# Two more scheduling passes and 24 hand-given leads and delays in an attention and mixture kernel's order of issue

## The chip, the cores and the metric

The kernel runs on one core of a Trainium2 chip. A time is the device time of one execution in microseconds (us). The kernel before was run three times, and its median is what the changed kernel is held against.

## The reference

Inputs are q, k and v (8 batches, 8 heads, 576 positions, 64 channels) and four weight matrices. Two attentions are added, and the sum goes through a gated feed-forward layer:

```python
q_d = q.reshape(B, H, 144, 4, D).mean(axis=3)         # k_d, v_d alike
out_up = np.repeat(softmax(q_d @ k_d.T / 8) @ v_d, 4, axis=2)
mask = abs(pos[:, None] - pos[None, :]) < 4           # seven neighbours
out_local = softmax(where(mask, q @ k.T / 8, -1e9)) @ v
x = (out_up + out_local).transpose(0, 2, 1, 3).reshape(4608, 512)
y = ((x @ w1) * (x @ w2) @ w3) @ w_out                # 512 -> 1024 -> 1024 -> 512
```

## The kernel before, in words

**The work.** The two last weights are multiplied with each other once (`fold`): 16 blocks of w3 (`block m hf`) and 8 blocks of w_out (`out_weight j`) are loaded, turned into float32 in three steps by ScalarE and VectorE (`words`: lines 301, 309 or 313, and 316), and 64 products (`product m j`, line 351, two MATMUL records each) build the folded weight `wphl`; `part m hf` issues them and copies a finished eighth out (lines 371, 372). The w1 and w2 blocks are loaded the same way (`gate_weights`; tiles w1a, w2a, wo, wb) and kept as a high and a low part.

The attention of a batch has a pooled part (`pooled b`, with `quad b qd`: scores into s_ps at line 482, exponentials at line 496, scaling at line 508, transposes into t_ps at line 521; then values into o_ps at line 449) and a local part in three units for each batch. In batches 0 and 1 (`PB`) the local part runs on TensorE: `group_unit n` calls `group_scores b j qd` (se_ps, line 655), its inner `rest` makes the transposes te_ps (line 626) and calls `group_values n` (oe_ps, line 697). The pooled sums of these batches are made by `pooled_sums b`, which loads q in 4 and k in 8 transfers (lines 553, 582) and adds them on VectorE. In batches 2 to 7 the local part runs on VectorE, ScalarE and POOL (`unit n`, VectorE's 128x768 products at line 767).

Two units make a chunk of 384 tokens; `moe c` runs it: for each of 8 slices f of the hidden layer 24 matmuls of 128x384 into the two banks pab (three matmuls for one product, lines 269 to 271, in float32r), ScalarE's copy of the first bank (line 912), VectorE's product with the second (line 914), the split into gh and gl (lines 919, 921), and `down f`: nine matmuls of 128x512 into acc. The end of a chunk copies acc out and stores it (lines 929, 942). There are 12 chunks.

**The order.** Every step is a `Task` with an engine, an assumed cost, its inputs and the buffers that it takes (`Ring`). Nothing runs while the list is made. `Plan.run` is a list scheduler on this graph: each engine takes, of its tasks that can start within `slack` of the earliest one, the one with the smallest priority; forward from the start or backward from the end (`back=True`). `Plan.order` alternates backward and forward passes (the start times of the one, negated, are the priorities of the next), tries 192 forward schedules, replays each with random delays, and keeps the one with the best mean. The tasks are then issued in its order, and each engine executes its own instructions in that order and waits by semaphores:

```python
self.best = min(found, key=lambda f: f[:2])[2]
self.mean = min(found)[0]
return [self.tasks[i] for i in self.best[3]]
```

SyncE's queue (SP) issues all loads of weights and inputs in plan order; POOL issues the accumulating transfers. A weight load needs one of 4 raw buffers (`early_raw`), a pooled batch's k load one of 2 (`k4`). Engines run their queues independently of each other.

Of the kernel before, what the change touches and what calls it, by code (L numbers as in the profile page):

```python
# [9 lines left out]
F32 = mybir.dt.float32  # L10
# [50 lines left out]
SEEDS = 4  # L61
ROUNDS = 8
AHEAD = 4

LOWS = dict(early=('ACT', 'ACT', 'DVE'), late=('ACT', 'DVE'))


class Ring:

    def __init__(self, n):  # L70
        self.n, self.held = n, []
# [6 lines left out]


class Task:  # L80
    __slots__ = ("eng", "cost", "fn", "deps", "late", "rings", "after")

    def __init__(self, eng, cost, fn, deps, late, rings, after):
        self.eng, self.cost, self.fn, self.deps, self.late, self.rings, self.after = eng, cost, fn, deps, late, rings, after


class Plan:

    def __init__(self):
        self.tasks = []  # L90

    def add(self, eng, cost, fn, deps=(), take=(), uses=(), late=0.0):

        got, rings, after = [], [], []
        for r in take:
            held, old, last = r.take()
            got.append(held)
            rings.append(old)
            after += last[:1]
        t = Task(eng, cost, fn, [d for d in deps if d is not None], late, rings, after)  # L100
        for h in list(got) + list(uses):
            h.append(t)
        self.tasks.append(t)
        return (t, *got) if take else t
# [71 lines left out]
    def replay(self, order, seed):  # L176
# [13 lines left out]
            end[i] = x  # L190
        return max(end)

    def order(self):


        self.link()
        n = len(self.tasks)
        far = [0.0] * n
        for i in reversed(range(n)):
            far[i] = self.tasks[i].cost + self.tasks[i].late + max([far[j] for j in self.suc[i]], default=0.0)  # L200
        found = []
        self.log = []
        for slow, spare in SLOW:
            now = self.run([-x for x in far], 0.05, slow=slow, spare=spare)
            for _ in range(ROUNDS):
                back = self.run([-x for x in now[2]], 0.05, back=True, slow=slow, spare=spare)
                tried = [self.run([-x for x in back[2]], z, slow=slow, spare=spare) for z in SLACKS]
                now = min(tried, key=lambda r: r[0])
                self.log.append((slow, spare, round(now[0], 1), round(min(sum(self.replay(r[3], k) for k in range(SEEDS)) / SEEDS for r in tried), 1)))
                found += [(sum(self.replay(r[3], k) for k in range(SEEDS)) / SEEDS, len(found) + i, r) for i, r in enumerate(tried)]  # L210
        self.best = min(found, key=lambda f: f[:2])[2]
        self.mean = min(found)[0]
        return [self.tasks[i] for i in self.best[3]]


def dve_us(n, fast=False):
# [23 lines left out]
def tile_attention_moe(ctx: ExitStack, tc: tile.TileContext, q, kw, vw, qk4, v4, w1, w2, w3, wout, edge, out):  # L240
# [78 lines left out]
    wo, folded = [None], []  # L319
    wo_ready, wp_ready, g_ready = {}, {}, {}  # L320

    def out_weight(j):
        def place():
            if wo[0] is None:
                wo[0] = wpool.tile([128, NF, DM], F32R, name="wo").bitcast(F32)
            return wo[0][:, j]
        _, ld, wo_ready[j], _ = words(wout[j].unsqueeze(1), place, [], "early")
        early.append(wo_ready[j])

    def fold():  # L330

        accs, held, xs, last = {}, {}, {}, {}
        start = {}

        def block(m, hf):
            T, _, tx, h = words(w3[m, hf].unsqueeze(1), lambda: pools["early"].tile([128, 512], F32, name="w3", bufs=BUFS["w3"]), [R["w3"]], "early")
            xs[m, hf] = T, tx, h

        def product(m, j):
            T, tx, h = xs[m, j // 4]  # L340
            three_of = m // 5
            shared = m not in (3, 4)

            def prod():
                if j == 0:
                    if not shared:
                        accs[m] = ps.tile([128, DM], F32, tag="ab", name="accw", bufs=BUFS["ab"])
                    elif m % 5 == 0:
                        for i in range(3):
                            accs[m + i] = ps.tile([128, DM], F32, tag="acc", name=f"accw{i}")  # L350
                nc.tensor.matmul(accs[m], lhsT=T["x"][:, j % 4 * 128:j % 4 * 128 + 128], rhs=wo[0][:, j], start=j == 0, stop=j == NF - 1)  # L351
            deps = [tx, last.get(m), wo_ready[j], start.get(three_of) if shared else None]
            ring = R["acc" if shared else "ab"]
            if j == 0 and (not shared or m % 5 == 0):
                t, held[m] = add("PE", 4 * mm_us(DM), prod, deps, take=[ring], uses=[h])
                if shared:
                    start[three_of] = t
                    held[m + 1] = held[m + 2] = held[m]
            else:
                t = add("PE", 4 * mm_us(DM), prod, deps, uses=[h, held[m]])  # L360
            last[m] = t

        def part(m, hf):
# [24 lines left out]
    def gate_weights(g):  # L388

        pool, users = ("early", early) if g < 2 else ("late", late)  # L390
        before = [] if g < 2 else list(early)
        n = 512 if g == 0 else 256
        at = (g - 1) * n if g else 0
        parts = 512 // n
        for wi, wsrc in enumerate((w1, w2)):
            for k0 in range(0, KT, parts):
                src = wsrc[min(g, 1), k0:k0 + parts, :, at:at + n].rearrange("k p n -> p k n")
                T, ld, tx, wx = words(src, lambda: pools[pool].tile([128, nw], F32, name="wx", bufs=BUFS[pool + "_wx"]), [R[pool + "_wx"]], pool, parts)
                ld.deps += before

                def high(T=T, wi=wi, k0=k0):
                    if gates[wi][g] is None:
                        both = [wpool, pools.get("wlate")][g - 1].tile([128, 2, KT, 2, n], F32R, name=["wo", "wb"][g - 1])
                        for i in range(2):
                            gates[i][g] = both[:, i]
                    T["p"] = gates[wi][g][:, k0:k0 + parts]
                    nc.scalar.copy(out=T["p"][:, :, 0], in_=T["x"].rearrange("p (k n) -> p k n", k=parts))
                th = add("ACT", act_us(nw), high, [tx] + (folded if g == 1 else []), uses=[wx])
                tl = add("DVE", dve_us(nw), lambda T=T: nc.vector.tensor_tensor(out=T["p"][:, :, 1], in0=T["x"].rearrange("p (k n) -> p k n", k=parts), in1=T["p"][:, :, 0].bitcast(F32), op=ALU.subtract), [th], uses=[wx])
                users += [th, tl]  # L410
                g_ready.setdefault((wi, g), []).extend([th, tl])


    oups, oup_ready, oup_held, raws = {}, {}, {}, {}
    pep = []

    def pooled(b):
        P = {}
        if b in PB:
# [48 lines left out]

    def quad(b, qd, P, lq, hq, hpt):
        T = {}

# [64 lines left out]

    fours, four_ready = {}, {}

    def pooled_sums(b):

        fours[b], four_ready[b] = {}, []
# [49 lines left out]
        pep.extend(done)  # L593
        return add("Pool", 0.0, lambda: None, done), hq

    def group_unit(n):
        b, j = divmod(n, NJ)
        c, u = divmod(n, 2)
# [16 lines left out]
        pep.extend(lvs)  # L615
        quads = [group_scores(b, j, qd, starts) for qd in range(2)]

        def rest():
            hpt = None
            pts = []  # L620
            for qd, (U, hs, no) in enumerate(quads):
# [18 lines left out]
            group_values(n, T, pts, hpt, lvs, hvs)  # L640
        return rest

    def group_scores(b, j, qd, starts):

        U = {}
# [36 lines left out]
        no = [add("DVE", dve_us(n2), lambda: nc.vector.tensor_tensor(out=p3(), in0=p3(), in1=wide_(U["sm"]), op=ALU.mult), [t], uses=[hs])]  # L682
        return U, hs, no

    def group_values(n, T, pts, hpt, lvs, hvs):

        b, j = divmod(n, NJ)
# [47 lines left out]
    chunks, x_ready, x_held = {}, {}, {}  # L735
    nq, nk = UT * D, (UT + W - 1) * D

    def unit(n):
        b, j = divmod(n, NJ)
        c, u = divmod(n, 2)  # L740
# [125 lines left out]
    per = lambda f: 4 if f < 4 else 2  # L866
    out_v = out.rearrange("(b k t) m -> b t k m", k=NB, t=BT)

    def moe(c):
        T = {}  # L870
        gated = []
# [17 lines left out]
                    lastd = add("PE", 3 * mm_us(DM), mmul, d, uses=[hg, hacc])  # L889

        for f in range(NF):
            ends, banks = [], []
            for which in range(2):
                t = None
# [27 lines left out]
            lag.append((f, [th, tl], hg))  # L922

        for f, d, hg in lag:
            down(f, d, hg)
        for i in range(3):
            def store_h(i=i):
# [27 lines left out]
    for n in range(NU):  # L955
        scores(n + 1)
        if n in rests:
            rests[n]()
        else:
            if n % NJ == 0:  # L960
                pooled(n // NJ)
            unit(n)
# [114 lines left out]
```

## Time and profile before

| what | value |
|---|---|
| three runs | 782.77, 783.5, 785.19 us; median 783.5 us |
| profiled execution | 783.63 us, of which the span from first to last instruction is 781.9 us |
| TensorE matmul (PE) busy | 752.5 us, 96% of the span |
| TensorE weight load (PEld) busy | 654.8 us, 84% |
| VectorE (DVE), ScalarE (ACT), POOL busy | 613.0, 540.0, 115.8 us |
| TensorE's mean granted clock | 0.993 of full speed |

The 1.7 us between span and time lie around the instructions. Busy shares are means over stages that differ, so the wait that ends last in a stage counts there. The matmuls' ends are modelled: a matmul of 128x384 is shown as 0.34 us long while the next starts 0.17 to 0.18 us later, so idle time between matmuls appears slightly too small.

### The profile page before, as it was taken

The page shows a single profiled execution, that of the slowest core. Times are in us where ns is not written, and L with a number is a line of the kernel's source. Part 1 is how long each engine was busy: PE and PEld are TensorE (multiplying, and loading weights), DVE is VectorE, ACT ScalarE, POOL GpSimd, SP SyncE. Part 2 cuts the span into 40 slices and gives each one's busy share as a digit, 9 for nine tenths or more (in the row PEclk, how much of TensorE's full clock was granted, in tenths as well). Part 3 has the DMA queues.
Part 4 walks back from the last instruction along what each step waited for, and adds up shares of the span by engine and source line. Part 5 has one row for each costly group of instructions (what it writes and reads, how often), then busy time and mean ns, then how long its engine had stood idle before and what let it go on. Part 6 is the DMA issues. An engine that isn't in the chain of part 4 may idle for free.

```text
span 781.9 us, 15058 instructions
## 1 busy us (share of the span) xinstructions
PE 752.5 (96%) x5320; PEld 654.8 (84%) x5320; DVE 613.0 (78%) x1049; ACT 540.0 (69%) x2120; POOL 115.8 (15%) x139
## 2 busy tenths in 40 slices
PE   4889999999999999999999999999999999999995
PEld 1445588898999899999999999998999999999994
DVE  4457966749999999989999998998998998963110
ACT  5788898647978688666787686776785787841211
POOL 1000011000221122211121222110221220110000
PEclk9999999999999999999999999999999999999998
DMA  8995779433576727856549739854469544350101
GB/s 291 305 252 182 230 190 218 81 104 103 117 181 177 149 63 202 202 99 171 127 88 224 172 80 216 169 119 135 119 134 224 122 114 120 63 100 1 41 0 41
DMA packets 42548, 111.92 MB, mean 143 GB/s; under 512 B 5080, under 2 KB 11224, under 8 KB 42472
## 3 DMA queue, kind: packets, MB, share of 16 engines
q0 software_dynamic: 12672, 38.94, 28.9%
q1 hardware_dynamic: 29800, 72.01, 28.5%
q8 instruction: 42, 0.69, 0.4%
q14 instruction: 34, 0.28, 0.1%
HBM read 80.26 MB, written 9.44 MB: 115 GB/s over the span
## 4 chain that ended last, share of the span: by engine, by line
PE 73%; issue 7%; DMA 7%; DVE 6%; ACT 5%; POOL 1%; SPq 1%; POOLq 0%; ACTq 0%; DVEq 0%
PE pab L269 14%; PE pab L270 14%; PE pab L271 14%; PE acc L269 7%; PE acc L271 7%; PE acc L270 7%; PE accw L351 3%; DMA raw<-in_w_dram 3%; PE t_ps L521 2%; DMA raw<-in_wout_dram 2%; PE o_ps L449 2%; ACT pexp L496 1%; DVE pr L767 1%; DMA xl<-pv 1%; PE s_ps L482 1%
## 5 line engine op out<-in xcount | busy, mean ns | idle before, releaser
L777 ACT ACTIVATE junk<-pr 128x64 f32<-128x64 f32 x432 | 110.8, 257 | 19.0 <-DVE pr L767 8.4
L767 DVE TENSOR_TENSOR pr<-q_t,kv 128x768 f32<-128x768 f32 x126 | 119.8, 973 | 3.6 <-DMA kv<-in_kw_dram 3.5
L826 ACT ACTIVATE pv<-kv,s_t 128x64 f32<-128x64 f32 x432 | 114.5, 342 | 10.3 <-DVE s_t L803 5.9
L269 PE MATMUL acc<-wphl,gh 128*128 128x512 f32 x288 | 115.5, 401 | 0.0
L271 PE MATMUL acc<-wphl,gl 128*128 128x512 f32 x288 | 113.8, 395 | 0.0
L270 PE MATMUL acc<-wphl,gh 128*128 128x512 f32 x288 | 113.6, 394 | 0.0
L912 ACT COPY a<-pab 128x384 f32<-128x384 f32 x96 | 45.9, 478 | 79.9 <-PE pab L271 66.5
L914 DVE TENSOR_TENSOR a<-pab,a 128x384 f32<-128x384 f32 x96 | 53.2, 554 | 53.5 <-PE pab L271 48.8
L842 POOL DMA_DIRECT2D xl<-pv x54 | 47.2, 875 | 311.4 <-DVE xl L844 249.7
L919 ACT CAST gh<-a 128x384 fp32r<-128x384 f32 x96 | 49.2, 513 | 59.4 <-PE acc L270 52.1
L780 DVE TENSOR_REDUCE s_t<-pr 128x12 f32<-128x768 f32 x90 | 84.1, 944 | 0.1
L777 ACT ACTIVATION_READ_ACCUMULATOR junk<-pr 128x1 f32 x432 | 81.1, 188 | 0.0
L351 PE MATMUL accw<-wo,w 128*128 128x512 f32 x128 | 64.4, 638 | 15.5 <-DVE w L316 12.2
L921 DVE TENSOR_TENSOR gl<-a,gh 128x384 fp32r<-128x384 f32 x96 | 53.9, 562 | 27.9 <-ACT gh L919 27.5
L834 DVE TENSOR_TENSOR pv<-kv,s_t 128x768 f32<-128x768 f32 x72 | 69.8, 979 | 0.1
L269 PE MATMUL pab<-xh,wo 128*128 128x384 f32 x192 | 66.3, 346 | 0.5 <-ACT a L912 0.5
L269 PE MATMUL pab<-xh,w2a 128*128 128x384 f32 x192 | 66.1, 344 | 0.3 <-DVE a L914 0.2
L269 PE MATMUL pab<-xh,w1a 128*128 128x384 f32 x192 | 66.2, 345 | 0.0
L269 PE MATMUL pab<-xh,wb 128*128 128x384 f32 x192 | 65.8, 343 | 0.2
L270 PE MATMUL pab<-xl,w2a 128*128 128x384 f32 x192 | 65.7, 342 | 0.0
L271 PE MATMUL pab<-xh,w2a 128*128 128x384 f32 x192 | 65.5, 341 | 0.0
L271 PEld LDWEIGHTS acc<-wphl,gl 128*128 128x128 f32 x288 | 54.1, 188 | 13.2
(109 smaller groups left out, 1718.6 us busy)
## 6 DMA issues: line engine op xcount, KB each, us to landing
xl<-pv POOLq DMA_DIRECT2D x54, 384.0 KB, 4.3
raw<-in_w_dram SPq DMA_DIRECT2D x32, 512.0 KB
qks<-in_qk_dram POOLq DMA_DIRECT2D x18, 576.0 KB, 7.4
kv<-in_kw_dram SPq DMA_DIRECT2D x18, 576.0 KB
kv<-in_vw_dram SPq DMA_DIRECT2D x18, 576.0 KB
vs<-in_v_dram POOLq DMA_DIRECT2D x24, 288.0 KB, 6.5
q_t<-in_q_dram SPq DMA_DIRECT2D x18, 384.0 KB
out_dram<-o_sb SPq DMA_DIRECT2D x24, 256.0 KB
```

The lines of the kernel that those rows point to most:

```text
L269: nc.tensor.matmul(out_ps, lhsT=lh, rhs=rh, start=first, stop=False)
L270: nc.tensor.matmul(out_ps, lhsT=lh, rhs=rl, start=False, stop=False)
L271: nc.tensor.matmul(out_ps, lhsT=ll, rhs=rh, start=False, stop=last)
L351: nc.tensor.matmul(accs[m], lhsT=T["x"][:, j % 4 * 128:j % 4 * 128 + 128], rhs=wo[0][:, j], start=j == 0, stop=j == NF - 1)
L767: (nc.gpsimd if o in share["qk_pool"] else nc.vector).tensor_tensor(out=T[o], in0=T["q"], in1=T["k"][:, o * D:o * D + nq].rearrange("p (t ...
L777: nc.scalar.activation(out=junk, in_=T[o][:, t], func=AF.Copy, accum_out=T["s"][:, t, o:o + 1])
L780: reds.append(add("DVE", dve_us(nq), lambda o=o: nc.vector.tensor_reduce(out=T["s"][:, :, o], in_=T[o], op=ALU.add, axis=AX.X), [tp], uses ...
L826: nc.scalar.mul(out=T["pv", o][:, tt], in_=T["v"][:, (tt + o) * D:(tt + o + 1) * D], mul=T["s"][:, tt, o:o + 1])
L834: nc.vector.tensor_tensor(out=T["pv", o], in0=T["v"][:, o * D:o * D + nq].rearrange("p (t d) -> p t d", d=D), in1=T["s"][:, :, o].unsqueez ...
L914: tg = add("DVE", dve_us(CT), lambda f=f: nc.vector.tensor_tensor(out=T["a", f], in0=T["p", 1, f], in1=T["a", f], op=ALU.mult), [ta, ends[ ...
L919: nc.scalar.copy(out=T["gh", f], in_=T["a", f])
L921: tl = add("DVE", dve_us(CT), lambda f=f: nc.vector.tensor_tensor(out=T["gl", f], in0=T["a", f], in1=T["gh", f].bitcast(F32), op=ALU.subtr ...
```

## The change

Each planning function is wrapped (`@plan.named`), so that every task carries the name of its group: the function and its whole-number arguments, with " SP" added for tasks of the SP engine; in `moe` the group is set by hand to `gates c f` and `down c f`. The body of the loop in `gate_weights` becomes a function, `gate_block g wi k0`, with the same tasks. `rest` gets n as an argument for its name alone. After the best of the 192 schedules is chosen as before, its start times become priorities; twice a forward pass, a backward pass (with 10% more transfer time) and a set of shifts follow: a negative number gives a group's tasks a lead, a positive one a delay. A last forward pass makes the order that is issued. No task, cost, buffer or instruction is added, removed or altered.

```diff
+SHIFTS = [
+    "",
+    "gates_0_1:4.5",
+    "block_0_1:14.5 block_1_1:-1 down_0_1:-7 down_0_2:-2.5 gate_block_0_0_2:-2.5 gate_block_2_0_0:8 gates_0_3:-6"
+    " group_scores_0_2_1:-3 group_scores_1_0_0:-11 group_scores_1_1_0:-19 group_scores_1_2_1:-3 group_values_2:-26.5"
+    " out_weight_4:-3 part_4_1:-2 pooled_2:2 pooled_sums_1_SP:-14 product_5_0:-1.5 product_6_4:-6.5 product_7_4:29"
+    " quad_0_1:3.5 quad_1_0:-13.5 quad_1_1:-7 rest_4:0.5",
+]
...
+        self.group = group + " SP" if eng == "SP" else group
...
+    def named(self, fn):
+
+        def run(*a):
+            old, self.group = self.group, " ".join([fn.__name__] + [str(x) for x in a if isinstance(x, int)])
+            r = fn(*a)
+            self.group = old
+            return r
+        return run
...
+    def again(self, prio):
+        now = self.run(prio, 0.1)
+        back = self.run([-x for x in now[2]], 0.05, back=True, slow=1.1)
+        return [-x for x in back[2]]
+
...
         self.mean = min(found)[0]
-        return [self.tasks[i] for i in self.best[3]]
+
+        prio = list(self.best[1])
+        for k, line in enumerate(SHIFTS):
+            if k:
+                prio = self.again(prio)
+            shift = dict((g.replace("_", " "), float(x)) for g, x in (w.split(":") for w in line.split()))
+            prio = [p + shift.get(t.group, 0.0) for p, t in zip(prio, self.tasks)]
+        self.final = self.run(prio, 0.1, slow=1.1)
+        return [self.tasks[i] for i in self.final[3]]
...
+            plan.group = f"gates {c} {f}"
...
+            plan.group = f"down {c} {f}"
...
-            rests[n]()
+            rests[n](n)
```

## Rows read from the trace of the kernel before

**Rows 1.** The page: busy time of each engine, share of the span, instructions
```profile
PE 752.5 (96%) x5320; PEld 654.8 (84%) x5320; DVE 613.0 (78%) x1049; ACT 540.0 (69%) x2120; POOL 115.8 (15%) x139
```
**Rows 2.** Windows: stretch, its length, busy time by engine, granted clock, DMA share, GB/s
```profile
0.00:8.31 8.31, 0.00 (x0) 0.00 (x1) 1.50 (x3) 3.96 (x6) 3.67 (x19) 1.00 0.73 259
8.31:46.00 37.69, 30.80 (x112) 12.71 (x112) 22.20 (x60) 25.93 (x63) 1.82 (x2) 1.00 0.98 302
46.00:98.00 52.00, 50.41 (x545) 27.21 (x546) 39.56 (x96) 43.83 (x121) 0.83 (x1) 1.00 0.71 213
98.00:106.00 8.00, 6.24 (x38) 5.25 (x40) 4.15 (x10) 7.74 (x21) 0.83 (x1) 0.79 0.81 256
106.00:200.00 94.00, 92.94 (x1073) 83.29 (x1066) 67.25 (x149) 68.85 (x267) 9.40 (x10) 1.00 0.50 126
200.00:560.00 360.00, 359.52 (x2278) 330.68 (x2277) 334.66 (x513) 272.25 (x1195) 72.80 (x78) 1.00 0.65 148
560.00:760.00 200.00, 200.00 (x1227) 184.78 (x1226) 141.50 (x219) 113.74 (x448) 26.41 (x28) 1.00 0.42 97
740.00:760.00 20.00, 20.00 (x105) 18.52 (x104) 3.35 (x6) 2.98 (x6) 0.00 (x0) 1.00 0.00 0
760.00:781.90 21.90, 12.56 (x63) 10.85 (x61) 2.23 (x4) 3.75 (x7) 0.00 (x0) 0.83 0.14 37
```
**Rows 3.** Timeline of PE, 13 to 47 us: start, length, what, [idle before <-releaser]
```profile
13.31 3.74 PE L351 MATMUL accw<-wo,w 128*128 128x512 f32 x4 [1.22 <-DVE wo L316]
18.73 7.13 PE L351 MATMUL accw<-wo,w 128*128 128x512 f32 x16 [1.68 <-DVE w L316]
...
28.82 5.42 PE L351 MATMUL accw<-wo,w 128*128 128x512 f32 x12 [2.06 <-DVE wo L316]
...
41.02 3.98 PE L351 MATMUL accw<-wo,w 128*128 128x512 f32 x8 [0.92 <-DVE w L316]
46.26 1.13 PE L351 MATMUL accw<-wo,w 128*128 128x512 f32 x2 [1.25 <-DVE w L316]
```
**Rows 4.** Timeline of the DMA issues on SP, 4 to 13 us and 78 to 84 us
```profile
4.30 7.67 SPq L582 DMA_DIRECT2D k<-in_qk_dram  x8
12.13 0.33 SPq L294 DMA_DIRECT2D raw<-in_w_dram  x1
...
78.77 2.08 SPq L582 DMA_DIRECT2D k<-in_qk_dram  x4
...
82.42 1.77 SPq L582 DMA_DIRECT2D k<-in_qk_dram  x4
```
**Rows 5.** Timeline of PE, 98 to 102 us
```profile
99.99 0.39 PE L521 MATMUL t_ps<-ident,pexp 112*72 112x112 f32 x2 [1.23 <-ACT pexp L508]
100.91 1.21 PE L521 MATMUL t_ps<-ident,pexp 112*72 112x112 f32 x10 [0.53 <-ACT pexp L508]
```
**Rows 6.** Timeline of ACT, 98 to 102 us
```profile
98.99 0.64 ACT L407 CAST w2a<-wx 128x512 fp32r<-128x512 f32 x1
99.50 1.97 ACT L508 ACTIVATE pexp<-pexp,grs 128x144 f32<-128x144 f32 x6
101.34 0.63 ACT L407 CAST w2a<-wx 128x512 fp32r<-128x512 f32 x1
```
**Rows 7.** Windows of tile pab alone, columns PE, PEld, DVE, ACT, clock, DMA
```profile
101.90:105.70 3.80, 3.80 (x12) 3.37 (x12) 0.00 (x0) 0.50 (x1) 0.55 1.04 357
106.60:108.80 2.20, 2.20 (x12) 2.20 (x13) 0.00 (x0) 0.00 (x0) 1.00 0.76 180
```
**Rows 8.** Groups by line on DVE: busy us, mean ns, idle before, releasers
```profile
L767 DVE TENSOR_TENSOR pr<-q_t,kv 128x768 f32<-128x768 f32 x126 | 119.8, 973 | 3.6 <-DMA kv<-in_kw_dram 3.5
...
L914 DVE TENSOR_TENSOR a<-pab,a 128x384 f32<-128x384 f32 x96 | 53.2, 554 | 53.5 <-PE pab L271 48.8 <-ACT junk L777 3.1 <-ACT a L912 0.9
```
**Rows 9.** Timeline of ACT, 770 us to the end
```profile
771.20 1.28 ACT L929 COPY o_sb<-acc 128x512 f32<-128x512 f32 x2 [1.62 <-PE acc L271]
775.90 0.58 ACT L929 COPY o_sb<-acc 128x512 f32<-128x512 f32 x1 [3.41 <-DMA out_dram<-o_sb]
```

More of the change, by code (lines that the diff above doesn't have):

```diff
@@ L80, with __init__ @@
 class Task:
-    __slots__ = ("eng", "cost", "fn", "deps", "late", "rings", "after")
-    def __init__(self, eng, cost, fn, deps, late, rings, after):
+    __slots__ = ("eng", "cost", "fn", "deps", "late", "rings", "after", "group")
+    def __init__(self, eng, cost, fn, deps, late, rings, after, group):
         self.eng, self.cost, self.fn, self.deps, self.late, self.rings, self.after = eng, cost, fn, deps, late, rings, after
+        self.group = group + " SP" if eng == "SP" else group
 class Plan:
@@ L90, in __init__ @@
         self.tasks = []
+        self.group = ""
+    def named(self, fn):
[5 more added lines that the diff above has]
+        return run
     def add(self, eng, cost, fn, deps=(), take=(), uses=(), late=0.0):
@@ L99, in add @@
             after += last[:1]
-        t = Task(eng, cost, fn, [d for d in deps if d is not None], late, rings, after)
+        t = Task(eng, cost, fn, [d for d in deps if d is not None], late, rings, after, self.group)
         for h in list(got) + list(uses):
@@ L320, in tile_attention_moe @@
     wo_ready, wp_ready, g_ready = {}, {}, {}
+    @plan.named
     def out_weight(j):
@@ L333, in fold @@
         start = {}
+        @plan.named
         def block(m, hf):
@@ L337, in block @@
             xs[m, hf] = T, tx, h
+        @plan.named
         def product(m, j):
@@ L361, in product @@
             last[m] = t
+        @plan.named
         def part(m, hf):
@@ L394, in gate_weights @@
         parts = 512 // n
-        for wi, wsrc in enumerate((w1, w2)):
-            for k0 in range(0, KT, parts):
[L397 to L411, printed above, removed]
@@ new lines, in gate_block, with high @@
+        @plan.named
+        def gate_block(g, wi, k0):
+            src = (w1, w2)[wi][min(g, 1), k0:k0 + parts, :, at:at + n].rearrange("k p n -> p k n")
+            T, ld, tx, wx = words(src, lambda: pools[pool].tile([128, nw], F32, name="wx", bufs=BUFS[pool + "_wx"]), [R[pool + "_wx"]], pool, parts)
+            ld.deps += before
+            def high():
+                if gates[wi][g] is None:
+                    both = [wpool, pools.get("wlate")][g - 1].tile([128, 2, KT, 2, n], F32R, name=["wo", "wb"][g - 1])
+                    for i in range(2):
+                        gates[i][g] = both[:, i]
+                T["p"] = gates[wi][g][:, k0:k0 + parts]
+                nc.scalar.copy(out=T["p"][:, :, 0], in_=T["x"].rearrange("p (k n) -> p k n", k=parts))
+            th = add("ACT", act_us(nw), high, [tx] + (folded if g == 1 else []), uses=[wx])
+            tl = add("DVE", dve_us(nw), lambda: nc.vector.tensor_tensor(out=T["p"][:, :, 1], in0=T["x"].rearrange("p (k n) -> p k n", k=parts), in1=T["p"][:, :, 0].bitcast(F32), op=ALU.subtract), [th], uses=[wx])
+            users.extend([th, tl])
+            g_ready.setdefault((wi, g), []).extend([th, tl])
@@ L414, in tile_attention_moe @@
+        for wi in range(2):
+            for k0 in range(0, KT, parts):
+                gate_block(g, wi, k0)
     oups, oup_ready, oup_held, raws = {}, {}, {}, {}
     pep = []
+    @plan.named
     def pooled(b):
@@ L467, in pooled @@
                 pep.append(t)
+    @plan.named
     def quad(b, qd, P, lq, hq, hpt):
@@ L539, in tile_attention_moe @@
     fours, four_ready = {}, {}
+    @plan.named
     def pooled_sums(b):
@@ L594, in pooled_sums @@
         return add("Pool", 0.0, lambda: None, done), hq
+    @plan.named
     def group_unit(n):
@@ L616, in group_unit, with rest @@
         quads = [group_scores(b, j, qd, starts) for qd in range(2)]
-        def rest():
+        @plan.named
+        def rest(n):
             hpt = None
@@ L641, in group_unit @@
         return rest
+    @plan.named
     def group_scores(b, j, qd, starts):
@@ L683, in group_scores @@
         return U, hs, no
+    @plan.named
     def group_values(n, T, pts, hpt, lvs, hvs):
@@ L736, in tile_attention_moe @@
     nq, nk = UT * D, (UT + W - 1) * D
+    @plan.named
     def unit(n):
@@ L867, in tile_attention_moe @@
     out_v = out.rearrange("(b k t) m -> b t k m", k=NB, t=BT)
+    @plan.named
     def moe(c):
```

## The prediction, made before the changed kernel was run

> **What bounds the kernel now.** I read the page first, for the fullest engine. PE is busy 752.5 us of 781.9 [rows 1]: 29.4 us lie without a matmul, and only these can be won by an order that leaves every instruction as it is. Where they lie is in the windows [rows 2]. The stretch before the first matmul is 8.31 us; 8.31 to 46 us holds 37.69 − 30.80 = 6.89 us of idle PE, 46 to 98 us 1.59, 98 to 106 us 1.76, 106 to 200 us 1.06, 200 to 560 us 0.48, 560 to 760 us nothing, and the end after 760 us 9.34. The reader should see that the 560 us from 200 to 760 us are solid, so that all that can be won lies in the first 200 us, and that a worse order can lose time in all 760.
>
> Second, what ends the early waits, by PE's timeline [rows 3]. Five waits of 1.22, 1.68, 2.06, 0.92 and 1.25 us before the products of the fold all end on VectorE's last step on a weight block. SP's timeline shows why the blocks are late at 13 to 19 us: eight issues of k loads hold SP for 7.67 us from 4.30 us, and the next weight load goes out only at 12.13 us [rows 4]. From 8.31 to 46 us the DMA engines are at a share of 0.98 [rows 2]: there is little spare transfer time, and a better order there can only exchange which load comes first.
>
> Third, the stall at 98 to 106 us. PE waits 1.23 and 0.53 us for ScalarE's scaling of the exponentials of batch 1's first pooled quad [rows 5]. Behind it the clock falls: 12 matmuls of pab take 3.80 us at a mean granted clock of 0.55 and 2.20 us at full clock just after [rows 7]. At 0.79 granted over the 8 us, 0.21 x 8 = 1.68 us of matmul time are lost there [rows 2], the 2.4 GHz level being left for 1.2 GHz for some 3.4 us. Together with the idle 1.76 us the place costs 3.44 us. It begins with a load: the k blocks of batch 1 are issued at 78.77 and 82.42 us [rows 4], and after their landing come VectorE's sums, the scores and the exponentials.
>
> PE's busy time could mislead, as its matmuls overlap in the record. PEld is busy 84% of the span [rows 1], but in the solid stretch 740 to 760 us, with PE never idle, it shows 18.52 of 20 us too [rows 2]. The Trainium skill ("Perfetto Trace Analysis", Identifying the Most-Contended Engine) calls matmul busy time no good measure of the distance to the roofline and wants the weight loads' busy share: by that some 781.9 − 654.8 = 127 us would be open, against 29.4 by the rows. This case's solid stretch speaks for the rows.
>
> **The change part by part.** Nothing is added or removed, so each edit is worth what its waits are worth. The `named` wrapper, the group names, `gate_block` and `rest(n)` change only how the list is written: no instruction, hence no time.
>
> *The stall at 98 to 106 us (3.44 us).* `pooled_sums_1_SP:-14` gives batch 1's 4 q and 8 k transfers a lead, `quad_1_0:-13.5` its exponentials and transposes, `group_scores_0_2_1:-3` the last scores of batch 0, which hold a k buffer. The DMA share over 46 to 98 us is 0.71 [rows 2], so earlier transfers find room; they would push v and raw loads back on SP by the 2.08 + 1.77 us that the k issues take [rows 4]. `quad_1_0` also goes before weight conversions on ScalarE: a conversion of 0.64 us stands ahead of the scaling of 1.97 us, another of 0.63 us behind it [rows 6]. `product_7_4:29` makes the fold's last four products (each waits for the one before) the last choice, so that PE has them for a wait. What is late next: the w2a matmuls behind the transposes need the conversion at 101.34 us. ScalarE is busy 7.74 of these 8 us [rows 2], so not all is won: between 0 and 3.44 us I take 2.4, about two thirds, as the scaling itself must still run once.
>
> *The fold's loads and blocks, 8 to 47 us.* The shifts `out_weight_4`, `block_0_1`, `block_1_1`, `quad_0_1`, `product_5_0`, `product_6_4`, `part_4_1` exchange blocks, of which the products of the last three waits [rows 3] can profit: 2.06 + 0.92 + 1.25 = 4.23 us. The first two (2.90 us) stand behind batch 0's k loads, whose group has no shift; only the repeated passes could move those. With transfers full [rows 2], I take 1.2 us of 4.23. If the first waits closed too, matmuls would also leave the slow start sooner (4 records in 3.74 us at 13.31 us, 16 in 7.13 us later [rows 3]: 0.94 against 0.45 us each); four records, some 2 us, are its bound, and I take nothing.
>
> *Groups of units 0 to 5 and chunk 0* (`rest_4`, `group_values_2`, the other `group_scores`, `quad_1_1`, `gates_0_1`, `gates_0_3`, `down_0_1`, `down_0_2`, `gate_block_0_0_2`, `gate_block_2_0_0`, `pooled_2`). They lie in 46 to 200 us, where 1.59 + 1.06 us of waits are left outside the stall [rows 2]. `group_values_2:-26.5` can act as a filler too. Of these 2.65 us I take 0.6 + 0.3 = 0.9.
>
> *The passes themselves.* The order that is issued is now the outcome of one last pass and not chosen among replays, and it is new for the whole kernel, not only for the named groups. After 200 us there is 0.48 us to win and much to lose. The nearest row for an order with some waits in dense work is 106 to 200 us: 1.06 us in 94, which over 560 us would be 6.3. Between a gain of 0.48 and a loss of 6.3 I take a loss of 1.0: VectorE, the likeliest cause, has 360 − 334.66 = 25 us free from 200 to 560 us [rows 2] to take up a different order.
>
> *First load and last store.* The 8.31 us before the first matmul are the first two blocks' way through load and conversion; neither has a shift. At the end ScalarE copies acc, and its third copy waits 3.41 us for a store [rows 9]; these all come after the last matmul, and an order can't move them. Both at nothing, with no cover needed.
>
> Sum: 2.4 + 1.2 + 0.9 − 1.0 = 3.5 us won. The profiled execution took 783.63 us (median of three: 783.5), so 783.63 − 3.5 = **780.1 us**, 0.43% below the median. A difference under 0.3%, 2.35 us, is about what a measurement of this kernel can't tell from none.
>
> **The rivals.**
>
> *All waits that the shifts can reach are closed*: 3.44 + 4.23 + 2.65 = 10.3 us, hence 773.3 us. For it: the shifts name work at each of these places. Against: transfers at 0.98 and ScalarE at 7.74 of 8 us [rows 2].
>
> *The wait only changes its name.* ScalarE's work in the crowded stretch is the same; if the scaling comes first, the w2a conversion at 101.34 us [rows 6] comes later, and PE waits on VectorE's low part of w2a instead of on the transposes. Then only some of the clock's 1.68 us is won and the fold's 1.2 us, less the loss of 1.0 later: 1.0 to 1.9 us, 782.2 us, no change that can be told.
>
> *Slower: PE's two pab banks are emptied late.* VectorE's product with the second bank (L914, 0.554 us, 96 of them) frees it. In 48.8 us of idle time before it VectorE waited for PE, so it often comes in time, and yet it shares its queue with 126 products of 0.973 us [rows 8]. PE has 12 matmuls for the other bank, 2.20 us [rows 7], before it needs this one; one VectorE operation ahead (0.97 + 0.55 = 1.5 us) is hidden, two (2.5) cost 0.3 us, three (3.5) 1.3 us. The new order decides for slower when six of 96 stand three deep: 7.8 us lost against 4.5 won gives 786.9 us. For it: VectorE is 93% busy from 200 to 560 us, and the last pass keeps no margin that replays would have shown. Against: before, PE loses 0.48 us there. The Trainium skill ("TensorE: Matmul & The Clock Gate", Architectural detail) says that matmuls stay in program order, only weight loads being pulled ahead, and that ScalarE and VectorE are strictly first in, first out. The trace agrees: PE stood 1.23 us [rows 5] with matmuls of w2a queued behind the transposes. By it nothing slips past a badly placed instruction, so this rival costs its full price.
>
> **How the numbers follow.** The forecast has a chance of 0.46, all reachable waits closed 0.09, the renamed wait 0.27, the late banks 0.18. Faster by over 0.3% (under 781.15 us) is the first two, 0.55; within 0.3% the third, 0.27; slower (over 785.85 us) the last, 0.18. The forecast's own bounds are 783.63 − 2.4 − 1.2 − 0.9 − 0.48 = 778.6 with no loss later, and 783.63 + 2.0 − 2.25 = 783.4 with twice the loss and half of the gains. The range of 774.0 to 786.5 us reaches close to the fully closed waits below and the late banks above; about one in ten is left out on each side.
>
> **What would show it.** Right: a chain with less idle PE at 98 to 106 us and a granted clock of 1.00 there, batch 1's k issues some microseconds before 78.77 us, four fold products after batch 1's first scores, idle PE of 5 to 6 us from 8.31 to 46 us, under 2 us of idle PE from 200 to 760 us, and an end after the last matmul as before. Wrong: idle PE in front of pab on `a` (L912, L914), of acc on gl, or of w2a on its conversion; a second fall of the clock; or a later first matmul. A median under 775 us would mean that the first two waits went as well.

## The result and the profile after

The changed kernel takes **787.02 us** (median of 11 runs, 784.04 to 790.24) against 783.5 us (11 runs, 781.55 to 785.62) of the kernel before. The ratio is 1.0048, with a 95% interval of 1.0025 to 1.0071: slower by 0.48%, where 0.43% faster was forecast, and outside the range of 774.0 to 786.5 us. The late banks, at 786.9 us, had a chance of 0.18.

The profiled execution of after took 784.87 us, a low one of its runs; its span is 783.1 us. It is read here and set beside two more profiles of the same kernel further down. After's lines stand some 30 to 50 below those of before: L301 to L303 are 269 to 271 (pab and acc), L964 is 914 (VectorE's product that frees a bank), L962 is 912, L971 is 921, L892 is 844 (VectorE's sum of a unit), L890 is 842 (POOL's accumulating transfer `xl<-pv`), L815 is 767, L386 is 351, L348 is 316 (VectorE's last step on a weight block), L563 is 521, L993 is 942 (a store), L794 to L802 are 746 to 754 (the loads of a unit).

The page's first part, and the windows of [rows 2] for after (columns as there):

```profile
PE 750.9 (96%) x5320; PEld 653.2 (83%) x5320; DVE 601.1 (77%) x1049; ACT 538.1 (69%) x2120; POOL 117.3 (15%) x139
```
```profile
0.00:8.31 8.31, 0.00 (x0) 0.00 (x0) 1.35 (x3) 4.18 (x7) 3.68 (x19) 1.00 0.73 260
8.31:46.00 37.69, 30.57 (x113) 13.10 (x113) 21.30 (x60) 24.60 (x59) 1.82 (x2) 0.95 0.94 300
46.00:98.00 52.00, 51.24 (x552) 28.20 (x553) 40.63 (x99) 47.34 (x124) 0.83 (x1) 1.00 0.73 225
98.00:106.00 8.00, 6.81 (x42) 5.99 (x40) 5.47 (x15) 8.00 (x26) 0.83 (x1) 1.00 0.74 205
106.00:200.00 94.00, 93.28 (x1079) 83.43 (x1079) 61.56 (x141) 64.46 (x248) 9.90 (x10) 1.00 0.49 124
200.00:560.00 360.00, 355.48 (x2252) 326.77 (x2251) 332.45 (x520) 273.89 (x1207) 72.49 (x78) 1.00 0.65 150
560.00:760.00 200.00, 199.72 (x1222) 183.77 (x1221) 136.06 (x214) 111.86 (x446) 27.70 (x28) 1.00 0.41 92
```

Two rows answer the prediction. From 98 to 106 us the granted clock is 1.00 where it was 0.79, and PE is idle 1.19 instead of 1.76 us. From 200 to 560 us PE is idle 4.52 us where it was 0.48. The first is the stall that was to close, the second the loss that was taken at 1.0 us.

The waits of PE from 200 to 760 us (engine, line, releaser: us in total, times, longest) name the second. First the one row of this view before, then the two of after:

```profile
PE pab L269 <- DVE a L914: 0.2, 1, 0.2
```
```profile
PE pab L301 <- DVE a L964: 4.4, 4, 2.2
PE pab L301 <- ACT a L962: 0.3, 1, 0.3
```

Two of after's four waits on VectorE make 3.9 of the 4.4 us. PE's timeline at the first, then at the second:

```profile
362.82 0.34 PE L303 MATMUL pab<-xh,wo 128*128 128x384 f32 x1
365.36 0.45 PE L301 MATMUL pab<-xh,wo 128*128 128x384 f32 x1 [2.20 <-DVE a L964]
...
427.24 0.34 PE L303 MATMUL pab<-xh,wb 128*128 128x384 f32 x1
429.28 0.45 PE L301 MATMUL pab<-xh,wb 128*128 128x384 f32 x1 [1.70 <-DVE a L964]
```

Why L964 was late shows VectorE's timeline at the same places:

```profile
359.84 0.55 DVE L971 TENSOR_TENSOR gl<-a,gh 128x384 fp32r<-128x384 f32 x1
363.88 0.96 DVE L892 TENSOR_TENSOR xl<-xl,pv 128x768 f32<-128x768 f32 x1 [3.49 <-DMA xl<-pv]
364.76 0.55 DVE L964 TENSOR_TENSOR a<-pab,a 128x384 f32<-128x384 f32 x1
...
426.81 0.96 DVE L815 TENSOR_TENSOR pr<-q_t,kv 128x768 f32<-128x768 f32 x1 [3.07 <-DMA q_t<-in_q_dram]
427.81 0.95 DVE L828 TENSOR_REDUCE s_t<-pr 128x12 f32<-128x768 f32 x1
428.67 0.55 DVE L964 TENSOR_TENSOR a<-pab,a 128x384 f32<-128x384 f32 x1
```

VectorE isn't too busy here; it stands idle 3.49 and 3.07 us on a transfer, with the product that PE needs one or two places behind. Such a wait alone doesn't stop PE. Before, VectorE waits as long at 486 us, but the next product that frees a bank stands ten places behind, and PE isn't idle from 480 to 500 us:

```profile
485.96 0.96 DVE L767 TENSOR_TENSOR pr<-q_t,kv 128x768 f32<-128x768 f32 x1 [3.51 <-DMA kv<-in_kw_dram]
...
494.23 0.55 DVE L914 TENSOR_TENSOR a<-pab,a 128x384 f32<-128x384 f32 x1
```

The transfer of the first place, by POOL's timeline and SP's:

```profile
354.44 0.86 POOL L890 DMA_DIRECT2D xl<-pv  x1 [13.72 <-DVE xl L892]
```
```profile
348.69 6.25 SPq L993 DMA_DIRECT2D out_dram<-o_sb  x4
355.06 0.79 SPq L794 DMA_DIRECT2D q_t<-in_q_dram  x1
355.90 3.97 SPq L798 DMA_DIRECT2D kv<-in_kw_dram  x1
359.92 1.61 SPq L802 DMA_DIRECT2D kv<-in_vw_dram  x1
```

The 384 KB accumulate, issued at 354.44 us, comes in 9.42 us later (the chain of waits shows it as one piece of that length); the median landing of the 54 is 4.6 us in this trace, 4.3 before. Four stores of 256 or 128 KB were issued just ahead and 1,536 KB of loads just behind. The Trainium skill ("DMA: Bandwidth & Descriptors", Issuing engines are not separate DMA queues) says that transfers of all issuing engines run on the same 16 DMA engines and interleave. The trace fits that: the accumulate from POOL took twice its median landing time between transfers from SP.

### The profile page after: what moved, and what is told of

The parts are those of the page before. It is cut to its first block, busy times and chain, and to the rows that moved or that the text cites. A ratio compares the mean times of both kernels' runs of the same rounds, so it can differ in the third digit from the quotient of the medians.

```text
span 783.1 us, 15041 instructions
## 1 busy us (share of the span) xinstructions
PE 750.9 (96%) x5320; PEld 653.2 (83%) x5320; DVE 601.1 (77%) x1049; ACT 538.1 (69%) x2120; POOL 117.3 (15%) x139
## 4 chain that ended last, share of the span: by engine, by line
PE 66%; DMA 14%; DVE 7%; issue 6%; ACT 4%; POOL 1%; SPq 0%; DVEq 0%; POOLq 0%; ACTq 0%
PE pab L301 13%; PE pab L302 12%; PE pab L303 12%; PE acc L301 6%; PE acc L303 6%; PE acc L302 6%; DMA xl<-pv 4%; PE accw L386 4%; DMA vs<-in_v_dram 3%; DMA raw<-in_w_dram 2%; DVE pr L815 2%; DMA q_t<-in_q_dram 2%; PE o_ps L490 2%; PE t_ps L563 2%; DMA out_dram<-o_sb 1%
## 5 line engine op out<-in xcount | busy, mean ns | idle before, releaser
L815 DVE TENSOR_TENSOR pr<-q_t,kv 128x768 f32<-128x768 f32 x126 | 120.0, 968 | 6.3 <-DMA q_t<-in_q_dram 5.5
L301 PE MATMUL acc<-wphl,gh 128*128 128x512 f32 x288 | 115.4, 401 | 0.0
L303 PE MATMUL acc<-wphl,gl 128*128 128x512 f32 x288 | 113.7, 395 | 0.4 <-DVE gl L971 0.4
L962 ACT COPY a<-pab 128x384 f32<-128x384 f32 x96 | 45.8, 477 | 73.7 <-PE pab L303 56.4
L964 DVE TENSOR_TENSOR a<-pab,a 128x384 f32<-128x384 f32 x96 | 53.0, 553 | 55.5 <-PE pab L303 52.6
L890 POOL DMA_DIRECT2D xl<-pv x54 | 47.5, 879 | 298.9 <-DVE xl L892 228.2
L971 DVE TENSOR_TENSOR gl<-a,gh 128x384 fp32r<-128x384 f32 x96 | 53.5, 557 | 32.7 <-ACT gh L969 32.5
L386 PE MATMUL accw<-wo,w 128*128 128x512 f32 x128 | 63.6, 635 | 14.6 <-DVE w L348 14.6
L301 PE MATMUL pab<-xh,wo 128*128 128x384 f32 x192 | 66.4, 346 | 2.2 <-DVE a L964 2.2
L301 PE MATMUL pab<-xh,wb 128*128 128x384 f32 x192 | 65.7, 342 | 2.2 <-DVE a L964 1.9
L301 PE MATMUL pab<-xh,w1a 128*128 128x384 f32 x192 | 66.2, 345 | 0.9 <-ACT a L962 0.9
L303 PEld LDWEIGHTS acc<-wphl,gl 128*128 128x128 f32 x288 | 54.1, 188 | 14.0 <-DVE gl L971 0.8
L301 PE MATMUL pab<-xh,w2a 128*128 128x384 f32 x192 | 65.3, 340 | 0.4 <-DVE a L964 0.3
L302 PE MATMUL pab<-xl,wo 128*128 128x384 f32 x192 | 64.9, 338 | 0.6 <-issue 0.6
```

Of the source, the lines that this page charges most:

```text
L301: nc.tensor.matmul(out_ps, lhsT=lh, rhs=rh, start=first, stop=False)
L302: nc.tensor.matmul(out_ps, lhsT=lh, rhs=rl, start=False, stop=False)
L303: nc.tensor.matmul(out_ps, lhsT=ll, rhs=rh, start=False, stop=last)
L815: (nc.gpsimd if o in share["qk_pool"] else nc.vector).tensor_tensor(out=T[o], in0=T["q"], in1=T["k"][:, o * D:o * D + nq].rearrange("p (t ...
L964: tg = add("DVE", dve_us(CT), lambda f=f: nc.vector.tensor_tensor(out=T["a", f], in0=T["p", 1, f], in1=T["a", f], op=ALU.mult), [ta, ends[ ...
L971: tl = add("DVE", dve_us(CT), lambda f=f: nc.vector.tensor_tensor(out=T["gl", f], in0=T["a", f], in1=T["gh", f].bitcast(F32), op=ALU.subtr ...
```

## The experiments

The theories, in words. The first: the last passes make a new order for the whole kernel, whose part after some 150 us loses more than its head wins, because VectorE meets late transfers in front of the product that frees a bank. The rivals: that the shifts do the harm and the passes none; that the head's gain is not there or not kept; that the depth of VectorE's queue alone, not a transfer, holds the bank. Letters in the expectations stand for these and for variants of them.

Each run is given as median and ratio to before with its 95% interval, and, for the stretch 200 to 760 us, the idle PE (560 us less PE's busy time there). That row for before is 0.48 us, for after 4.80.

**The changed kernel again**, twice, with no edit.

> The changed kernel once more, unaltered, for a second profile. Theory A (the new order runs ahead in the first 150 us and loses that and more after 200 us, where VectorE's instructions that wait for a transfer stand ahead of those that free TensorE's banks, so that each late transfer stalls TensorE): 784 to 790 us, idle PE from 200 to 760 us of 3 to 9 us, in front of pab on the tile a, but at other places or of other lengths than 2.4 us at 363 us and 1.9 us at 427 us, since transfers land at other times in each execution. Theory B (the order has fixed flaws, the same in each execution): the same two stalls at the same places and of the same length, and times within 1 us of each other.

> The changed kernel unaltered, a third profile, for the head alone: where the 145th matmul of the gates and the second layer starts (133.8 us in the first profile, 136.7 us in the second, 138.2 us before). If the head's gain differs by execution: between 133 and 138 us; if the first profile was typical: 133.5 to 134.5 us. The stalls at 363 and 427 us again.

Measured: 788.21 us, 1.0068 (1.0043 to 1.0093); the third profile 786.26 us. Idle PE from 200 to 760 us: 3.89 and 3.62 us. Both have the two stalls of the first profile, at the same two products: 2.37 and 1.52 us in the second, 2.37 and 1.25 in the third. The accumulate at the first place is late each time: 9.60 and 9.61 us from its issue to VectorE's sum. So the stalls are fixed in the order, as theory B of the first expectation has it, and don't wander with each execution, as theory A had it. (The times within 1 us of each other that B also expected are not met: the runs go from 784.04 to 793.91 us.) The head does differ: the 145th matmul of pab and acc starts at 133.76, 136.70 and 135.49 us in the three profiles. The windows around the first place and PE's timeline, in the second profile:

```profile
364.00:372.00 8.00, 5.63 (x24) 5.27 (x23) 5.08 (x12) 1.33 (x5) 3.29 (x3) 0.79 0.75 224
367.40:370.80 3.40, 3.07 (x10) 3.07 (x11) 3.40 (x11) 0.27 (x1) 2.86 (x3) 0.50 0.81 198
```
```profile
367.73 0.69 PE L301 MATMUL pab<-xh,wo 128*128 128x384 f32 x1 [2.37 <-DVE a L964]
```

Here the stall also costs the clock: 0.50 granted over 3.40 us, 1.7 us of matmul time, as the old stall at 98 us did before. The third profile shows the same (0.79 over these 8 us), the first does not (1.00). So the place costs 2.2 us in one execution and some 4.1 in two.

**The kernel before again**, a second profile.

> The kernel before once more, a second profile of it: the 145th such matmul at 137.5 to 139.5 us, under 1 us of idle PE from 200 to 760 us.

Measured: 784.53 us; idle PE from 200 to 760 us 0.34 us; the 145th matmul at 139.11 us. The stalls belong to the changed order.

**The passes without shifts**, and **the last pass alone**:

```diff
 SHIFTS = [
     "",
-    "gates_0_1:4.5",
-    "block_0_1:14.5 block_1_1:-1 ... rest_4:0.5",
+    "",
+    "",
 ]
```
```diff
+SHIFTS = [""]
```

> The two passes and the last one, with no group shifted. Theory A (what costs is that the order is the outcome of the last pass and no longer the one that lost least in the replays): slower than before as well, 785 to 790 us, idle PE of 3 us or more from 200 to 760 us. Rival (the 24 shifts cause the loss): 782 to 785 us, as before, with under 1 us of idle PE from 200 to 760 us. Both expect less of a gain in the first 150 us than the 4.2 us that the changed kernel is ahead there.

> The start times of the best schedule as priorities, then the last forward pass alone: no further pass, no shift. If leaving the choice among replays is what costs: as slow as the kernel with the two passes and no shift, 786 to 791 us, with waits for late transfers after 200 us. If the two further passes cost: 783 to 785 us, nearly the order of before.

Measured: 789.39 us, 1.0071 (1.0048 to 1.0095), idle PE 5.80 us; and 795.1 us, 1.0131 (1.0101 to 1.0161), idle PE 4.71 us. Without any shift the kernel is slower than before too, and with the last pass alone by far the slowest. (Of that run's 11.3 us at the 3,025th matmul of pab and acc 3.2 are there at the 433rd; behind it PE waits 2.4 us for POOL, 1.6 for ScalarE's copy L957 and 0.5 for VectorE: a poorer order altogether, not the same two places.) With the passes alone the longest wait, 2.48 us at 372.03 us, is for ScalarE's copy of the first bank, and the same accumulate stands behind it: VectorE waits 4.44 us for it, ScalarE 4.69 us for VectorE, and the copy stands behind in ScalarE's queue.

```profile
368.50 0.96 DVE L889 TENSOR_TENSOR xl<-xl,pv 128x768 f32<-128x768 f32 x1 [4.44 <-DMA xl<-pv]
```
```profile
369.64 0.27 ACT L840 ACTIVATE s_t<-s_t 128x84 f32<-128x84 f32 x1 [4.69 <-DVE s_t L839]
```

The shifts are not the harm: with them the time is 2.4 us below the passes alone (787.02 against 789.39), or 1.2 by the second set of runs, a gain that this spread of runs doesn't set clear of nothing.

**Head and tail apart.** Each engine takes the tasks that start early from one order and the rest from the other:

```diff
-        return [self.tasks[i] for i in self.final[3]]
+        head = {i for i in self.best[3] if self.best[1][i] < 150.0}
+        mixed = [i for i in self.final[3] if i in head] + [i for i in self.best[3] if i not in head]
+        return [self.tasks[i] for i in mixed]
```

So the new head goes with the old tail; `final` and `best` exchanged gives the old head with the new tail, and 120.0 or 330.0 for 150.0 moves the seam.

> The tasks that the schedule of before starts in its first 150 us are issued in the changed order, all others in the order of before. Theory A: the head's gain stays and the tail's loss is gone, 4.2 us less than before, 779 to 781 us, with under 1 us of idle PE after 200 us. Rival (a faster head itself makes the later loads collide and costs the gain back): 784 to 787 us, with the stalls after 200 us again.

> The reverse: the tasks that the changed schedule starts in its first 150 us are issued in the order of before, all others in the changed order. Theory A: none of the gain and all of the loss, 5 us or more over before, 787 to 793 us, idle PE after 200 us of 3 us or more. Rival (the faster head makes the collisions): 783 to 785 us, with under 1 us of idle PE after 200 us.

> As the kernel with the changed order of the first 150 us, but cut at 120 us. If what lost the head's gain there was the stall without a visible cause at 137 us and the fall of the clock behind it: no such stall in the profile, 2 to 4 us less than before, 779.5 to 781.5 us. If a faster head always gives its gain back at the seam: 783 to 785 us.

> The changed order for all tasks that the schedule of before starts in its first 330 us, ahead of the stalls at 363 and 427 us; all others in the order of before. If those stalls and what follows are all that the changed order loses: the head's gain, 2.0 us on the mean of five profiles, stays, and 781 to 782.5 us come out, with under 1 us of idle PE from 400 to 760 us. If a seam costs what the head gains, or the order of before also suffers when it starts from another state: 783.5 to 787 us.

Measured:

| head, tail, seam | median us | ratio (95%) | idle PE 200 to 760 us |
|---|---|---|---|
| new, old, 150 us | 783.88 | 1.0002 (0.9979 to 1.0025) | 1.75 |
| old, new, 150 us | 787.98 | 1.0053 (1.0032 to 1.0074) | 3.74 |
| new, old, 120 us | 784.21 | 1.0006 (0.9991 to 1.0022) | 0.94 |
| new, old, 330 us | 789.34 | 1.0074 (1.0048 to 1.0100) | 4.94 |

The tail alone brings the whole loss (1.0053 against 1.0048 and 1.0068); the head alone wins nothing that shows, where 779 to 781 us were expected. That it wins nothing is less clear than it looks. The new head was ahead by 3.59 us at the 145th matmul of pab and acc (with 24 small matmuls, some 0.6 us, still to come that the order before had issued); then, close before the seam at 150 us, PE's timeline and the window have

```profile
137.45 0.44 PE L303 MATMUL pab<-xh,wo 128*128 128x384 f32 x1
139.77 0.34 PE L304 MATMUL pab<-xl,wo 128*128 128x384 f32 x1 [1.89 <-issue]
```
```profile
139.00:144.00 5.00, 4.23 (x34) 3.27 (x34) 1.12 (x4) 1.46 (x8) 0.83 (x1) 0.66 0.54 115
```

a wait for nothing that the profile shows ("issue"), and a fall of the clock behind it. What it is stays open, and it isn't the seam's own: after and its third profile have 0.58 and 0.85 us of it near this place, the passes alone 1.03 and the two swaps below 1.40, the profiles of before none. With the seam at 120 us it isn't there, and the time is no better; that profile is ahead by only 0.4 us at the 145th matmul. The seam at 330 us was a miss: it was to keep the head's gain up to there, and its profile had lost it at 60 us already, on a late load (at its seam, 333 to 340 us, it lost 3.6 us more):

```profile
59.49 2.77 PE L492 MATMUL o_ps<-pt,vs 72*32 72x144 f32 x64 [2.14 <-DMA vs<-in_v_dram]
```
```profile
60.00:68.00 8.00, 8.00 (x109) 4.33 (x100) 1.78 (x4) 2.46 (x5) 0.00 (x0) 0.57 0.43 139
```

**The suspected transfers left out**, in the changed kernel and in the kernel before. The 54 accumulates `xl<-pv` on POOL are not issued, so that half of the products `pv` doesn't reach the sum; all else is as it was:

```diff
-  t = add("Pool", 1.04, lambda o=o: nc.gpsimd.dma_start(out=T["x"], in_=T["pv", o], accum_op=ALU.add), [t, tm], ...
+  t = add("Pool", 1.04, lambda: None, [t, tm], ...
```

> The changed order with the 54 accumulating transfers into xl left out (three of seven neighbours' terms are then missing from the local attention of batches 2 to 7), the place of each in the plan kept. Theory C (the stalls at 363 and 427 us come from transfers that land later than the plan assumes, since they share the engines with loads issued after them; VectorE waits for them and TensorE's bank stands behind): no idle PE over 1 us at 363 us, idle PE from 200 to 760 us under 2 us, and the changed order then ends 2 to 5 us ahead of the same cut in the order of before. Theory B' (the order of VectorE's own work after 200 us is what is bad): at least 3 us of idle PE left there and the changed order still behind the order of before.

> The order of before with the same 54 transfers left out, to compare with. All theories: 780 to 783.5 us, since PE was idle for 0.5 us only from 200 to 760 us; the fold and the first 150 us hold none of these transfers.

Measured: 781.7 us, 0.9983 (0.9959 to 1.0007), idle PE 0.28 us; and 782.61 us, 0.9987 (0.9970 to 1.0004), idle PE 0.01 us. Without the accumulates the changed order wins 6.5 us on its own 788.21, the order before 1.4 on 784.0. The loss after 200 us is gone: the changed order is 0.9 us ahead, which is within the noise and less than the 2 to 5 us expected, where it was 3.5 to 4.2 behind. That VectorE's queue is too deep by itself falls with this: its instructions are all still there, in the same order. VectorE's waits for transfers from 200 to 760 us, in after and with the accumulates left out:

```profile
DVE xl L892 <- DMA xl<-pv: 12.9, 7, 3.5
DVE pr L815 <- DMA q_t<-in_q_dram: 5.5, 3, 3.1
...
DVE pr L815 <- DMA kv<-in_kw_dram: 0.9, 1, 0.9
```
```profile
DVE pr L815 <- DMA kv<-in_kw_dram: 1.1, 1, 1.1
```

Before, they are 6.7 us in 4 waits on accumulates and one of 3.5 on a kv load. The waits for q_t go as well, although those loads are still issued: their lateness hung on the accumulates, in the transfers or by what VectorE did later. The run doesn't separate the two, as it takes 54 x 384 KB of transfers away together with the waits on them.

**The two places mended.** At the two stalls the transfer-waiting instruction, with what follows it up to the product, is put behind the product that frees the bank: three VectorE instructions of 1,049 change places.

```diff
+        for free, first in (("gates 4 4", "unit 11"), ("gates 5 5", "unit 15")):
+            tg = [t for t in dve if t.group == free][0]
+            p = dve.index(tg)
+            k = max(i for i in range(p) if dve[i].group == first and any(d.late for d in dve[i].deps))
+            for t in dve[k:p]:
+                order.remove(t)
+            at = order.index(tg) + 1
+            order[at:at] = dve[k:p]
```

> The changed order with three of VectorE's instructions moved at two places: at 364 us the addition that waits for an accumulating transfer goes behind the product that frees a pab bank, at 427 us the first product and reduction of a unit, which wait for the load of q, go behind the next such product. Theory C (the bank stands behind a late transfer in VectorE's queue): the stalls of 2.4 to 2.8 and 1.3 to 1.9 us are gone, also the fall of the clock behind the first, 3 to 5 us less than the changed kernel: 783 to 785 us. Rival (PE is held by what VectorE does over longer stretches, and any order that starts these late stalls soon after): the same idle PE from 200 to 760 us at other places, 786 to 789 us.

Measured: 785.57 us, 1.0014 (0.9994 to 1.0035), idle PE 2.71 us. PE's waits from 200 to 760 us are now

```profile
PE pab L312 <- DVE a L975: 1.9, 2, 1.6
PE pab L312 <- ACT a L973: 0.4, 1, 0.4
PE acc L314 <- DVE gl L982: 0.2, 1, 0.2
```

Both stalls are gone, 4.4 us of waits on VectorE's product have become 1.9, and the median is 1.5 to 2.6 us below the changed kernel's two (787.02 and 788.21). It ends half way between the two expectations. The cause at the two places is shown, and 1.6 us of it turned up again at the next bank, some microseconds behind the first place. What the swap is worth in time is shown less well: the intervals of the ratios overlap, and the profile, of an execution of 788.5 us, loses nearly as much behind the head as the changed kernel's (4.1 us, table below), of which 2.2 are more idle PE than before.

No version ran ahead of the kernel before with its whole work; the two with the new head up to 120 or 150 us equal it.

## Why the prediction was wrong

The start times of the pab and acc matmuls (3,168 records) show where an order is ahead. At the 433rd and at the 3,025th every order has issued the same other matmuls too. Against before's 209.1 us at the one and 744.0 us at the other:

| profile | at the 433rd | at the 3,025th | lost between |
|---|---|---|---|
| after | −4.07 | +1.22 | 5.3 |
| changed, second | −1.92 | +2.83 | 4.8 |
| changed, third | −2.06 | +2.34 | 4.4 |
| changed, two swaps | +0.43 | +4.55 | 4.1 |
| old head, new tail | +0.03 | +3.05 | 3.0 |
| passes alone | −2.59 | +5.63 | 8.2 |
| changed, no accumulates | −0.83 | −1.77 | −0.9 |
| before, no accumulates | +0.51 | −1.13 | −1.6 |
| before, again | +0.81 | +0.53 | −0.3 |

**The step that failed is "The passes themselves".** It took a loss of 1.0 us between a gain of 0.48 and a loss of 6.3; three profiles show 4.4 to 5.3. Its ground was that VectorE has 25 us free from 200 to 560 us [rows 2]. The free time is there, but it doesn't help: VectorE spends it standing on a transfer, and what is queued behind stands too. A second term failed by nearly as much, the gain of the first 200 us: 4.5 us were taken, 1.3 to 3.1 measured (below). With only one of the two wrong, 781.5 to 784 us would have come out, inside the range. The rival *PE's two pab banks are emptied late* had the right place, the right sign and nearly the right time (786.9 us). That the time fits is luck, as it is made of 4.5 us won and 7.8 lost; and in one thing the rival had the wrong reason: not six places three instructions deep, but two with a transfer 3 us late ahead of the product. A depth of 1.5 to 2.5 us, counted from [rows 8], PE's other bank covers or nearly covers; a wait of 3 us on top it doesn't. The prediction's price for a place, 0.3 to 1.3 us, so became 1.3 to 2.4, and up to 4.1 with the clock. The range, too, was narrower than its own chances: its upper end of 786.5 us lies under this rival's 786.9, which had 0.18 and not one in ten.

**The stall at 98 to 106 us was right.** 2.4 us were taken. Its 1.68 us of lost clock and 0.57 of 1.76 us idle came back, 2.25 us. The other two profiles of the changed kernel have a clock of 1.00 there as well (idle 1.01 and 0.80 us), the second of before 0.81 (1.69). The way was another one than forecast: the k loads of batch 1 go out at 78.54 and 81.88 us, hardly earlier than in [rows 4], and the transposes of [rows 5] simply come later, behind the matmuls of w1a and w2a, and find their input ready:

```profile
103.71 0.34 PE L303 MATMUL pab<-xh,w2a 128*128 128x384 f32 x1
103.88 1.37 PE L563 MATMUL t_ps<-ident,pexp 112*72 112x112 f32 x12
```

So a different filler was found for PE, not a shorter wait for ScalarE, and not the fold's last products: these are through at 95 us, and some stood behind batch 1's first scores before as well.

**The fold, 8 to 47 us, went another way.** 1.2 us of idle PE were taken; PE is busy 30.57 us there instead of 30.80. In place of the waits of 1.22 and 1.68 us of [rows 3] stands one of 4.39, and the last three, 4.23 us before, have shrunk to two of 0.69 and 1.05:

```profile
18.34 9.69 PE L386 MATMUL accw<-wo,w 128*128 128x512 f32 x18 [4.39 <-DVE w L348]
...
38.17 1.98 PE L386 MATMUL accw<-wo,w 128*128 128x512 f32 x4 [0.69 <-DVE w L348]
...
45.91 2.41 PE L386 MATMUL accw<-wo,w 128*128 128x512 f32 x5 [1.05 <-DVE w L348]
```

The clock falls behind the first, 0.50 over 18.87 to 22.28 us. By idle PE the stretch won nothing. By the work that is done it did: the first matmul of pab, with the same 648 other matmuls behind it in every profile, starts at 94.94, 96.59 and 95.50 us in the three of the changed kernel and at 96.09 and 97.62 in the two of before, some 1.2 us earlier on the mean. How much of that is the fold's stays open.

**Groups of units 0 to 5.** 0.9 us were taken; idle PE falls by 0.83 us from 46 to 98 us and by 0.34 from 106 to 200, in this profile about as forecast. The other two don't show it: 2.96 and 2.84 us are idle in these two stretches together, and 2.65 and 3.41 in the two profiles of before. For the head varies from run to run: the six profiles with the changed head and no seam before 200 us that were taken (after, its second and third, two swaps, no accumulates, the seam at 330 us with +2.49) are ahead by 1.0 us on the mean at the 433rd matmul, four with the old head (before, again, new tail, no accumulates: 0, 0.81, 0.03, 0.51) behind by 0.3. The gain is so 1.3 us, with an uncertainty of about 1; by the three unaltered profiles against the two of before it is 3.1. By neither is it 4.5. One cause is the late v load above; whether it is all stays open.

**First load and last store** were right: the first matmul starts at 8.51 us (8.31 before), and ScalarE's third copy of the end still waits 3.41 us, as in [rows 9].

The sum with what was measured: 1.3 to 3.1 us won at the head less some 4.8 lost behind gives 1.7 to 3.5 us slower, 785.2 to 787.0 us; the median of 787.02 lies at its upper end.

**Passes or shifts.** The prediction gave the shifts the gains and the passes a small loss. The passes alone lose 5.4 us (789.39 against 784.0), the shifts seem to give 1 to 2 back. What the change leaves out is the choice by replays with random delays: in these passes a transfer has a fixed time, and the order counts on it. The plan also lets transfers run one after the other in order of issue, so that loads issued behind an accumulate cost it nothing there. That either is why the two places came about is argued, not shown; no run chose the last pass by replays.

## What to carry to other kernels

When an order is made anew, look first for the instructions that wait for a transfer, and count what stands behind each in its queue: the free time of the engine is no cover where the engine spends it in such a wait. An instruction that empties a buffer of the bounding engine belongs ahead of one that waits for a transfer; three swapped instructions took away both stalls here, and by the medians some 2 us, which the spread of the runs doesn't set clear. Profile such an order more than once before calling a late transfer chance: here it was late in each execution. And a gain in one stage shown by one profile of a kernel whose head moves by some microseconds from run to run is not yet a gain: take several profiles, and compare where the same matmul starts.

## What was not expected of the hardware

An accumulating transfer of 384 KB took 9.42 us to land among stores and loads, at a DMA share of 0.78 over that time, against a median of 4.6 us; in two more executions VectorE had its sum 9.60 and 9.61 us after the issue. The windows of after for it:

```profile
354.44:363.86 9.42, 8.72 (x44) 7.59 (x43) 5.95 (x11) 7.58 (x36) 0.86 (x1) 1.00 0.78 182
```

In before the like one was issued at 352.31 us and VectorE had its sum at 359.30 us, 6.99 us later at a share of 0.81. The engines were not fuller when it took longer. One store was issued close to it, at 352.58 us, where after has four just ahead; that this is the cause is not shown.

Whether a stall costs the clock did not follow from its length. Behind 2.37 us at 367.73 us the level fell from 2.4 to 1.2 GHz for 3.4 us, behind 1.89 us at 139.77 us as well; behind 2.20 us at 365.36 us (clock 1.00 from 364 to 372 us), and behind 2.62 us in the run with the new tail, it stayed at 2.4 GHz:

```profile
369.96 0.44 PE L303 MATMUL pab<-xh,wo 128*128 128x384 f32 x1 [2.62 <-DVE a L966]
```
